# Order of loads, conversions and block requests in the first strip of a linear-attention and squared-ReLU MLP kernel

## The chip, the cores and the metric

The kernel runs on one core of a Trainium2 chip. The metric is the device time of one execution in microseconds. In the text PE is TensorE, DVE is VectorE, ACT is ScalarE, POOL is GpSimd and SP is SyncE, which here only issues DMAs.

## The reference

```python
kv = einsum('bhsd,bhse->bhde', k, v)        # q, k, v: (8, 8, 576, 64), float32
out = einsum('bhsd,bhde->bhse', q, kv)
rms = sqrt(mean(out * out, axis=-1, keepdims=True) + 1e-6)
x = (out / rms * g_norm)                    # heads joined: x is (4608, 512)
h = maximum(x @ w_in, 0.0)                  # w_in (512, 2048), float64
y = (h * h) @ w_out                         # w_out (2048, 512), float64
```

## The kernel before

**Tiling.** The 4608 tokens are cut into nine strips of 512 (`s` = 0 to 8). A strip has an up stage (x times `w_in`, squared ReLU into `gt`) and a down stage (times `w_out`, then a store). Strip 0 computes its up stage plainly (`up_first`, four matmuls of 512 columns for each of sixteen tiles) and its down stage with seven products in place of eight blocks (`down`, products 1 to 7, each in two halves; the order in strip 0 is 1, 2, 5, 6, 7, 3, 4). Strip 1 uses seven products in its up stage too, and from its down stage on each product is itself made of seven (`down_deep`, `up_slot`). These products need sums and differences of blocks of the weights and of x, which DVE and POOL make.

**Attention.** A batch has eight heads, taken as four pairs. For a pair, `transposed_query` (T) turns q on PE, `key_value` (K) multiplies k and v, and the query product follows. Its squares are summed (`mean_of`), ACT takes the root (`root_of`), DVE inverts it and takes a Newton step (`inverse_root`), and a multiply on DVE gives `x_n`, which PE transposes into `xT` (`features`).

**The opening.** The first 512 tokens, all of batch 0, go through steps of their own, listed by hand in `slices`: T, K, Q (`first_queries`: product, squares and mean), N (`first_normalized`: root, inverse and `x_n`), F (`first_features`), U (`first_up`: the first matmuls of the up stage), and for the weights `act` and `piece`. `w_in` and `w_out` come as float64 in pieces of 512 KB (`raw`). `convert_on_act` does two ACT operations on a piece, then `conversion` four DVE operations (L261, L263, L267, L270). `(piece, (i, n))` does the next n of these four for piece i. `keep_busy(ps, n)` makes n dummy matmuls (each two in the trace). Every engine runs its instructions in the order in which the program lists them.

**Loads.** Nearly all loads are issued by SP, in program order. `load(b, p, ...)` issues q, k and v of a pair, 256 KB each in batch 0; those of pairs 2 and 3 of batch 0 are put into a `gt` buffer (`first_qkv`). `load_piece` issues the next weight piece and `load_more` fills up to eight.

**Blocks of `w_out`.** The converted sums of `w_out` lie in DRAM. Products 1, 2 and 5 of strip 0 find their blocks in SBUF; for 6, 7, 3 and 4, in this order, `stream()` requests the next 1 MB block (`w_blk`, L824). It takes one of four buffers of `stream_pool`. `store_deep_sums(p, w)` makes four DVE sums of block p (`w_t`) for the deeper products of later strips and stores them (L857; those of product 6 use other buffers, L851). Its tiles come from the same four buffers. `deep_due` holds what is due, and the main loop empties it after each step except after one:

```python
while deep_due and i != n_up + 1:
    store_deep_sums(*deep_due.popleft())
```

In that loop `i - n_up` counts the halves of strip 0's down stage: 0 and 1 are product 1, 2 and 3 product 2, 4 and 5 product 5, 6 and 7 product 6, and so on. `attend` advances the `slices` of batch 1 between these steps; at `n_up + 5` it does the mean, root and norm of a pair of token tiles, whose `features` follow at `n_up + 7`.

Of the kernel before, what the change touches and what calls it, by code (L numbers as in the profile page):

```python
# [10 lines left out]
FP32 = mybir.dt.float32  # L11
# [9 lines left out]
def kernel(  # L21
# [34 lines left out]
    nc = tc.nc  # L56
    P = 128
# [4 lines left out]
    NP = H // 2  # L62
    FC = d_ff // P
    C = S // P
# [22 lines left out]
    g_pool = ctx.enter_context(tc.tile_pool(name="g", bufs=4))  # L87
# [10 lines left out]
    ctx.enter_context(tc.manual_schedule())  # L98


    main = {}

    def load(b, p, q_eng, names="kvq", parts=range(4)):
        hs = slice(2 * p, 2 * p + 2)
        inputs = (("q", q, q_eng), ("k", k, nc.sync), ("v", v, nc.sync))
        if b == 0 and p >= 2:

            h_place = g_pool.tile([P, 4, C * P], FP32, name="first_qkv", tag="gt")
        if b == 1 and p == 2:
            h_place = spare_pool.tile([P, 3, C * P], FP32, name="more_qkv")  # L110
        placed = (b, p) in ((0, 2), (0, 3), (1, 2))
        for i, (n, src, eng) in enumerate(inputs if b == 0 else inputs[1:] + inputs[:1]):
            if n not in names:
                continue
            whole = src[b, hs, 0 : C * P].rearrange("h (sp c) d -> sp h c d", c=C)
            if n == "q" and b >= Q_ON_PE:

                t = qkv_pool.tile([P, 4 * C, SQ], FP32, name=n, tag=n, bufs=3) if 0 in parts else main[n, b, p]
                for a in parts:
                    h, f = divmod(a * SQ, D)  # L120
                    eng.dma_start(
                        out=t[ts(a, SQ)],
                        in_=src[b, 2 * p + h, 0 : C * P, f : f + SQ].rearrange("(k i) f -> i k f", k=4 * C),
                    )
            elif n != "q":
                if placed:
                    t = h_place[:, i].rearrange("p (h c d) -> p h c d", h=2, c=C)
                else:
                    t = qkv_pool.tile([P, 2, C, D], FP32, name=n, tag=n)
                eng.dma_start(out=t, in_=whole)  # L130
            elif b == 0:

                if placed:
                    t = h_place[:, i].rearrange("p (h c d) -> p h c d", h=2, c=C)
                else:
                    t = qkv_pool.tile([P, 2, C, D], FP32, name=n, tag=n, bufs=3)
                eng.dma_start(out=t, in_=whole)
            else:

                if placed:  # L140
                    t = h_place[:, i].rearrange("p (c h d) -> p c h d", h=2, c=C)
                else:
                    t = qkv_pool.tile([P, C, 2, D], FP32, name=n, tag=n, bufs=3)
                for h in range(2):
                    eng.dma_start(out=t[:, :, h, :], in_=whole[:, h])
            main[n, b, p] = t
# [32 lines left out]
    to_load = iter(units)  # L179

    def load_next(q_eng=nc.sync, names="kvq"):
        u = next(to_load, None)
        if u is not None:
            load(*u, q_eng, names)
# [49 lines left out]
    def load_piece():  # L234
        if len(raw) < len(sources):
            t = raw_pool.tile([P, 2, WN // 2], I64, name="raw", tag="raw")
            nc.sync.dma_start(out=t, in_=sources[len(raw)])
            raw.append(t)
# [42 lines left out]
    def load_more(end):  # L281

        while len(raw) < min(end + 8, max(len(sources) - 4, end + 4), len(sources)):
            load_piece()
# [60 lines left out]

    load_next()
    load_rest(0, nc.sync)
    for p in range(1, NP):
        load_next()
        load_piece()  # L350
    load_more(0)
    g_col = const.tile([P, 1], FP32, name="g_col")
    g_src = g_norm.rearrange("(d u) -> d u", u=1)
# [13 lines left out]
    def keep_busy(ps, n):  # L367


        for _ in range(n):  # L370
            nc.tensor.matmul(ps, lhsT=ident, rhs=ident[:, : ps.shape[1]], start=True, stop=True)
# [38 lines left out]
    def key_value(b, *ps_of):  # L410
        while any(f == load and a[:2] == (b, p) or f == load_rest and a[0] == b for _, f, a in keys_due for p in ps_of):
            _, f, a = keys_due.popleft()
            f(*a)
        ps = apsum.tile([P, len(ps_of), D], FP32, name="kv_ps", tag="at")
        if (b, ps_of[0]) == (0, 0):
            keep_busy(ps[:, 0], 5)
            warm = apsum.tile([P, NT, P], FP32, name="x_ps", tag="first")[:, 0]
        half = slice(REST * (b % 2), REST * (b % 2 + 1))
        tiles = [[main.pop((n, b, p)) for n in "kv"] for p in ps_of]
        steps = [(i, c) for i in range(len(ps_of)) for c in range(C)] + [(i, C) for i in range(len(ps_of))]  # L420
        for i, c in steps:
            if (b, ps_of[i], c) == (0, 0, C):
                keep_busy(warm, 2)
            for h in range(2):
                at = (slice(None), h, c) if c < C else (half, 2 * ps_of[i] + h)
                a, w = (t[at] for t in (tiles[i] if c < C else (k_rest, v_rest)))
                nc.tensor.matmul(  # L427
                    ps[ts(h, D), i], lhsT=a, rhs=w, start=i == 0 and c == 0, stop=c == C, skip_group_check=True
                )
        at = (NP * b + ps_of[0]) % (2 * NP)  # L430
        d = kv_all[:, at : at + len(ps_of)]
        nc.scalar.copy(d[0:D, :, 0:D], ps[0:D])
        nc.scalar.copy(d[D:P, :, D:P], ps[D:P])
        for i, p in enumerate(ps_of):
            kvd[b, p] = d[:, i]
            if b < 2:
                if b == 1 and p == 0:
                    load_next()
            else:
                u = next(to_load, None)  # L440
                if u is not None:
                    keys_later(load, *u, nc.sync, "kv")
                if p == NP - 1 and b + 1 < B:
                    keys_later(load_rest, b + 1, nc.sync)
# [189 lines left out]
    slices, ready = [], {}  # L634
# [2 lines left out]
        convert_on_act, transposed_query, key_value, first_queries, first_normalized, first_features, first_piece  # L637
    )
    U = first_up
    slices += [(T, (0, 0)), (K, (0, 0)), (T, (0, 1)), (Q, (0,)), (K, (0, 1)), (N, (0,)), (act, (0,)), (piece, (0, 4))]  # L640
    slices += [(T, (0, 2)), (Q, (1,)), (F, (0,)), (K, (0, 2)), (N, (1,)), (act, (1,)), (U, (0, [0])), (piece, (1, 4))]
    slices += [(T, (0, 3)), (Q, (2,)), (F, (1,)), (U, (0, [1])), (K, (0, 3)), (N, (2,)), (act, (2,))]
    slices += [(Q, (3,)), (U, (0, [2])), (F, (2,)), (U, (1, [0])), (piece, (2, 1)), (N, (3,)), (act, (3,))]
    slices += [(piece, (2, 3)), (U, (1, [1, 2])), (F, (3,)), (piece, (3, 4))]
    slices += [(U, (2, [0, 1, 2])), (U, (3, [0, 1, 2]))]
    ready[0] = len(slices)
# [13 lines left out]
    T, K, last = transposed_query, key_value, query_pairs(1)[2]  # L660
# [198 lines left out]
    def down(s, p, i):  # L859
        if i == 0:  # L860
            open_bank(p)
        a = {1: 11, 2: 21, 6: 11, 7: 12, 3: 21, 4: 22}.get(p)
        w = w_blk[s, p]
        product(
            p, i,
            lambda fc: (gq[s, 1, fc // 2][:, fc % 2] if p == 5 else gq[s, a][:, fc])[:, ts(i, P)],
            lambda fc: w[:, :, fc], FQ,
        )

        if i == (p == 1) and s == DEEP - 1:  # L870
            deep_due.append((p, w))
        if i == 0:
            return
        del w_blk[s, p]

        if s == 0 and p in (2, 6, 3):
            reserve({2: 5, 6: 7, 3: 4}[p])
        if p not in (1, 7) and (s, p) not in ((0, 3), (0, 4)):
            stream()
        if p == (1 if s else 2):  # L880
            for g in range(NG):
                x = gq[s, 11][:, ts(g, 2)]
                minus(nc.vector, x, gq[s, 1, g], x)
        if p == (2 if s else 6):
            minus(nc.vector, gq[s, 21], gq[s, 21], gq[s, 11])

        def store(th, eh):
            def f(b, a=None):
                o = out_tile()
                if a is None:  # L890
                    nc.scalar.copy(o, b)
                else:
                    nc.vector.tensor_tensor(out=o, in0=b, in1=a, op=ALU.add)
                send(s, th, eh, o)
            return f

        combine(p, store(0, 0), store(0, 1), store(1, 0), store(1, 1))
# [284 lines left out]
    for s in range(N_STRIP):  # L1182
# [23 lines left out]
        for i, (w, fn, a) in enumerate(steps):  # L1206
# [53 lines left out]
                    stream()  # L1260
                continue
            if i == n_up:
                stream()
            if i == n_up + 3:
                store_first(2)
            if i in (n_up + 8, n_up + 11):
# [8 lines left out]
            n = i + 1 - (n_up - 6)  # L1275
            pairs, m = divmod(max(n - 2 * NP, 0), 3)
            attend(min(ready[0] + min(max(n, 0), 2 * NP) + (n >= 2 * NP) + 4 * pairs + (0, 2, 2)[m], goal))
            while deep_due and i != n_up + 1:
                store_deep_sums(*deep_due.popleft())
            if 11 <= i < n_up:  # L1280

# [31 lines left out]
```

## Time and profile before

| | us |
|---|---|
| median of 3 runs | 898.0 (897.18 to 898.66) |
| profiled execution, own time | 897.15 |
| its span | 895.1 |
| PE busy | 880.4 |
| DVE busy | 734.5 |
| ACT busy | 315.7 |
| POOL busy | 307.1 |
| DMA queue of SP, share of the 16 DMA engines' span | 81.2% |

The span runs from the first to the last instruction that the profiler saw; 2.05 us of the execution lie around it. Busy times are of one execution and overlap. All times named in the text as "at 118" are microseconds from the start of the span. The opening reaches to about 30 us, strip 0's up stage to 85, its down stage from 85 to 142, strip 1's up stage to 199.

### The profile page before, as it was taken

The numbers are of one execution on the slowest core, as the hardware profiler recorded it, in microseconds if no ns is written. First come the engines' busy times: TensorE is split into PE (matmuls) and PEld (weight loads), VectorE is DVE, ScalarE is ACT, GpSimd is POOL, SyncE is SP. The second block draws the span as 40 slices with busy tenths as digits, with TensorE's granted clock in tenths as the row PEclk, the third lists the DMA queues.
The fourth block names the chain that finished last, engine by engine and source line by source line (L and its number), as shares of the span: only waits on it lengthen the run. The fifth ranks groups of instructions, "written<-read, shape, count | busy, mean of one in ns | idle before, by whom it ended". The sixth has DMA issues, their size and how long they took to land.

```text
span 895.1 us, 20697 instructions
## 1 busy us (share of the span) xinstructions
PE 880.4 (98%) x8300; PEld 823.0 (92%) x8300; DVE 734.5 (82%) x1256; ACT 315.7 (35%) x622; POOL 307.1 (34%) x315
## 2 busy tenths in 40 slices
PE   8999999999999999999999999999999999999998
PEld 7445878889999999999999999999999999999998
DVE  3999999779779986898689966895899779875886
ACT  4798241320027302640255023801271027102710
POOL 0000005700558233632373035604460447044700
PEclk9999999999999999999999999999999999999999
DMA  9998998999988798969877989798748865884384
GB/s 303 307 316 250 310 330 267 289 314 323 313 197 279 266 326 238 277 249 317 250 232 238 323 239 248 237 297 292 218 143 297 304 203 164 301 299 154 128 316 180
DMA packets 169231, 235.71 MB, mean 263 GB/s; under 512 B 79408, under 2 KB 134192, under 8 KB 160688
## 3 DMA queue, kind: packets, MB, share of 16 engines
q1 hardware_dynamic: 168976, 234.40, 81.2%
q8 instruction: 65, 1.06, 0.5%
q14 instruction: 30, 0.25, 0.1%
q10 hardware_dynamic: 160, 0.00, 0.0%
HBM read 197.66 MB, written 36.70 MB: 262 GB/s over the span
## 4 chain that ended last, share of the span: by engine, by line
PE 74%; DVE 13%; DMA 6%; issue 2%; ACT 2%; SPq 2%; DVEq 0%; ACTq 0%
PE ps_B L944 22%; PE ps_A L944 17%; PE ps_A L1132 15%; PE ps_B L1132 8%; PE ps_A L729 4%; PE ps_C L1132 3%; PE ps_B L729 2%; PE kv_ps L427 1%; DVE w_c L267 1%; PE x_ps L463 1%; DVE gt L1144 1%; DMA w_blk<-w_in_deep 1%; DVE w_t L287 1%; DMA v_rest<-in_v_dram 1%; DMA x_d<-x_q 1%
## 5 line engine op out<-in xcount | busy, mean ns | idle before, releaser
L944 PE MATMUL ps_B<-w_blk,g_s 128*128 128x128 f32 x1024 | 126.2, 275 | 0.0
L944 PEld LDWEIGHTS ps_B<-w_blk,g_s 128*128 128x128 f32 x1024 | 120.0, 192 | 0.2
L1132 PE MATMUL ps_A<-x_l,w_in 128*128 128x128 f32 x784 | 104.1, 276 | 0.0
L287 POOL TENSOR_TENSOR x_l<-xT 128x256 f32<-128x256 f32 x21 | 16.2, 769 | 246.4 <-PE ps_A L944 246.4
L944 PE MATMUL ps_B<-w_blk,gt 128*128 128x128 f32 x768 | 97.4, 275 | 0.0
L1132 PEld LDWEIGHTS ps_A<-x_l,w_in 128*128 128x128 f32 x784 | 95.4, 192 | 0.5 <-DVE gt L1144 0.2
L944 PE MATMUL ps_A<-w_blk,g_s 128*128 128x128 f32 x768 | 93.6, 275 | 0.0
L944 PEld LDWEIGHTS ps_B<-w_blk,gt 128*128 128x128 f32 x768 | 91.5, 192 | 0.1
L944 PEld LDWEIGHTS ps_A<-w_blk,g_s 128*128 128x128 f32 x768 | 89.6, 192 | 0.0
L1144 POOL TENSOR_TENSOR snap<-snap,gt 128x512 f32<-128x512 f32 x35 | 46.6, 1332 | 118.9 <-ACT snap L1149 54.7
L1149 ACT COPY snap<-ps_A 128x512 f32<-128x512 f32 x63 | 36.7, 583 | 133.5 <-PE ps_A L1132 119.5
L1082 ACT ACTIVATE gt<-gt 128x512 f32<-128x512 f32 x112 | 69.6, 622 | 18.1 <-DVE gt L1144 18.0
L959 DVE TENSOR_TENSOR o_sb<-o_sb,ps_B 128x256 f32<-128x256 f32 (+1 forms) x128 | 49.5, 387 | 30.9 <-ACT o_sb L960 19.2
L944 PE MATMUL ps_A<-w_blk,gt 128*128 128x128 f32 x576 | 72.3, 275 | 0.0
L1083 ACT ACTIVATE gt<-gt 128x512 f32<-128x512 f32 x112 | 70.6, 631 | 3.6
L944 PEld LDWEIGHTS ps_A<-w_blk,gt 128*128 128x128 f32 x576 | 68.2, 192 | 0.4 <-DMA w_blk<-w_deep 0.2
L1144 POOL TENSOR_TENSOR gt<-gt,snap 128x512 f32<-128x512 f32 x42 | 52.6, 1278 | 23.8 <-DVE snap L1144 23.7
L287 DVE TENSOR_TENSOR gt<-gt 128x2048 f32<-128x2048 f32 (+1 forms) x29 | 59.7, 2063 | 0.0
L1042 POOL TENSOR_TENSOR w_i<-w_in 128x512 f32<-128x512 f32 x7 | 9.7, 1382 | 142.2 <-DVE w_in L287 141.5
L960 ACT COPY o_sb<-ps_A 128x128 f32<-128x128 f32 x24 | 6.4, 266 | 146.2 <-PE ps_A L944 146.2
L1132 PE MATMUL ps_A<-x_l,w_blk 128*128 128x128 f32 x392 | 52.2, 276 | 1.3 <-issue 1.2
L1132 PE MATMUL ps_B<-x_l,w_blk 128*128 128x128 f32 x392 | 52.0, 276 | 0.0
(180 smaller groups left out, 1811.7 us busy)
## 6 DMA issues: line engine op xcount, KB each, us to landing
w_blk<-w_deep SPq DMA_DIRECT2D x56, 1024.0 KB, 6.8
w_blk<-w_out SPq DMA_DIRECT2D x56, 768.0 KB, 6.0
w_blk<-w_in_deep SPq DMA_DIRECT2D x49, 768.0 KB, 4.8
raw<-in_moe_w_in_dram SPq DMA_DIRECT2D x16, 512.0 KB, 7.4
raw<-in_moe_w_out_dram SPq DMA_DIRECT2D x16, 512.0 KB, 6.2
k<-in_k_dram SPq DMA_DIRECT2D x29, 256.0 KB, 4.8
v<-in_v_dram SPq DMA_DIRECT2D x29, 256.0 KB, 5.0
x_d<-x_q SPq DMA_DIRECT2D x27, 256.0 KB, 5.3
```

The source lines that it names most:

```text
L267: yield nc.vector.scalar_tensor_tensor(out=ci, in0=high, scalar=-(2**30), in1=ci, op0=ALU.bitwise_and, op1=ALU.bitwise_or)
L287: eng.tensor_tensor(out=out, in0=a, in1=b, op=ALU.subtract)
L427: nc.tensor.matmul(ps[ts(h, D), i], lhsT=a, rhs=w, start=i == 0 and c == 0, stop=c == C, skip_group_check=True)
L729: nc.tensor.matmul(bank[BANK[p]][:, i, :], lhsT=lhsT(k), rhs=rhs(k), start=p in (1, 5, 2) and i == 0 and k == 0, stop=k == n - 1, skip_gro ...
L944: nc.tensor.matmul(chain[c][x][:, i, :], lhsT=a[:, f, :], rhs=w[:, f, :], start=x not in opened[c] and f == 0, stop=f == FQ // 2 - 1, skip ...
L959: add = lambda out, a, b: nc.vector.tensor_tensor(out=out, in0=a, in1=b, op=ALU.add)
L1042: nc.gpsimd.tensor_tensor(out=s1, in0=w_half(b, 0, 1), in1=w_half(b, 1, 1), op=ALU.add)
L1082: nc.scalar.activation(o, o, AF.Relu)
L1083: nc.scalar.activation(o, o, AF.Square)
L1132: nc.tensor.matmul(ps[:, i, :], lhsT=w, rhs=rhs, start=j in (1, 2, 5) and i == 0, stop=True, skip_group_check=True)
L1144: add = lambda eng, out, a, b: eng.tensor_tensor(out=out, in0=a, in1=b, op=ALU.add)
L1149: nc.scalar.copy(t, ps)
```

## The change

It has six parts. `load` remembers the `gt` buffer of a pair, so that q can be loaded apart from k and v. The first loads of pair 1 are no longer followed by a weight piece; for pairs 2 and 3 the order becomes q, piece, k and v in place of q, k, v, piece. The dummy matmuls before the first `key_value` go from five calls to three. In `slices`, the last DVE step of pieces 0 and 1 is put behind the mean of the next pair, and three of the `U` steps move. In strip 0's down stage two blocks are requested at `n_up` in place of one, one more at `n_up + 6`, and none any more in `down` of products 5 and 6. The loop no longer makes deep sums after step `n_up + 4`; they follow a step later, after that step's `attend`.

```diff
-    main = {}
+    main, first_places = {}, {}
...
         if b == 0 and p >= 2:
-            h_place = g_pool.tile([P, 4, C * P], FP32, name="first_qkv", tag="gt")
+            if p not in first_places:
+                first_places[p] = g_pool.tile([P, 4, C * P], FP32, name="first_qkv", tag="gt")
+            h_place = first_places[p]
...
     load_next()
     load_rest(0, nc.sync)
-    for p in range(1, NP):
-        load_next()
+    load_next()
+    for p in range(2, NP):
+        load(0, p, nc.sync, "q")
         load_piece()
+        load(0, p, nc.sync, "kv")
+        next(to_load)
     load_more(0)
...
-            keep_busy(ps[:, 0], 5)
+            keep_busy(ps[:, 0], 3)
...
-    slices += [(T, (0, 0)), (K, (0, 0)), (T, (0, 1)), (Q, (0,)), (K, (0, 1)), (N, (0,)), (act, (0,)), (piece, (0, 4))]
-    slices += [(T, (0, 2)), (Q, (1,)), (F, (0,)), (K, (0, 2)), (N, (1,)), (act, (1,)), (U, (0, [0])), (piece, (1, 4))]
-    slices += [(T, (0, 3)), (Q, (2,)), (F, (1,)), (U, (0, [1])), (K, (0, 3)), (N, (2,)), (act, (2,))]
-    slices += [(Q, (3,)), (U, (0, [2])), (F, (2,)), (U, (1, [0])), (piece, (2, 1)), (N, (3,)), (act, (3,))]
+    slices += [(T, (0, 0)), (K, (0, 0)), (T, (0, 1)), (Q, (0,)), (K, (0, 1)), (N, (0,)), (act, (0,)), (piece, (0, 3))]
+    slices += [(T, (0, 2)), (Q, (1,)), (F, (0,)), (K, (0, 2)), (piece, (0, 1)), (N, (1,)), (act, (1,)), (piece, (1, 3))]
+    slices += [(T, (0, 3)), (U, (0, [0])), (Q, (2,)), (F, (1,)), (U, (0, [1])), (K, (0, 3)), (piece, (1, 1)), (N, (2,))]
+    slices += [(act, (2,)), (U, (0, [2])), (Q, (3,)), (F, (2,)), (U, (1, [0])), (piece, (2, 1)), (N, (3,)), (act, (3,))]
...
-        if p not in (1, 7) and (s, p) not in ((0, 3), (0, 4)):
+        if p not in (1, 7) and (s, p) not in ((0, 5), (0, 6), (0, 3), (0, 4)):
             stream()
...
             if i == n_up:
-                stream()
+                stream(2)
...
-            while deep_due and i != n_up + 1:
+            if i == n_up + 6:
+                stream()
+            while deep_due and i not in (n_up + 1, n_up + 4):
                 store_deep_sums(*deep_due.popleft())
```

## The prediction

> **What bounds the kernel now.** I read the page's busy times first, then PE's waits, longest first (engine and what it writes, what it waited for; us in total, times, longest). PE is busy 98% of an 895.1 us span, so only its holes can give time:
>
> ```profile
> PE 880.4 (98%) x8300; PEld 823.0 (92%) x8300; DVE 734.5 (82%) x1256; ACT 315.7 (35%) x622; POOL 307.1 (34%) x315
> ```
>
> ```profile
> PE ps_A L576 <- DVE w_in L270: 1.8, 2, 1.1
> PE xt_ps L591 <- DVE x_n L531: 1.3, 2, 1.0
> PE ps_B L729 <- DVE w_in L287: 1.0, 1, 1.0
> PE t_ps L399 <- DMA first_qkv<-in_q_dram: 0.8, 1, 0.8
> PE x_ps L541 <- ACT kv_all L433: 0.5, 1, 0.5
> ```
>
> The reader sees that five waits of 5.4 us in all lie where the diff works: 1.8, 0.8 and 0.5 in the opening, 1.0 (of the 1.3) and 1.0 in the first strip's down stage. The third is misnamed: the block for product 3 is requested at 117.72 and takes 10.3 us, so it lands at 128.02, and PE starts at 128.16. It waits for that DMA. Next the windows, for what lies beside PE between the two places:
>
> ```profile
> 44.00:52.00 8.00, 8.00 (x20) 3.56 (x19) 8.00 (x18) 7.55 (x16) 0.00 (x0) 1.00 1.11 314
> 52.00:60.00 8.00, 8.00 (x20) 3.59 (x19) 8.00 (x19) 7.67 (x17) 0.00 (x0) 1.00 0.98 365
> 112.00:120.00 8.00, 7.04 (x36) 5.81 (x36) 7.44 (x16) 2.29 (x4) 0.00 (x0) 1.00 1.05 352
> ```
>
> After the stretch and its length come PE, PE's loads, DVE, ACT, POOL, clock, DMA share and GB/s. From 44 to 60 us four resources are full at once (PE 8.00 of 8, DVE 8.00, ACT 7.6, DMA about 1): time won earlier must get past each of them. From 112 to 120 PE loses 0.96 while DVE is at 7.44 of 8. The timeline shows how tight that is:
>
> ```profile
> 53.61 0.68 ACT L249 ACTIVATE w_c<-raw 128x512 f32<-128x512 f32 x1
> 55.40 0.66 ACT L777 ACTIVATE gt<-ps_B 128x256 f32<-128x256 f32 x2
> 56.39 3.60 PE L770 MATMUL ps_B<-xT,w_in 128*128 128x512 f32 x8
> ...
> 153.44 0.69 DVE L792 TENSOR_TENSOR gt<-ps_A,snap 128x512 f32<-128x512 f32 x1 [0.48 <-PE ps_A L729]
> ...
> 158.85 0.63 PE L591 MATMUL xt_ps<-ident,x_n 128*128 128x128 f32 x4 [0.34 <-DVE x_n L531]
> ```
>
> A PE tile of the first strip can start only when ACT has emptied the bank used four tiles before: ACT ends at 55.40 + 0.66 = 56.06, PE starts at 56.39, slack 0.33. And DVE, full from 26 us, first waits for PE at 153.44; at 158.85 PE waits for DVE.
>
> **What the skill says.** "TensorE: Matmul & The Clock Gate", What's actually happening: PE starts at half clock and is released after some 3.4 us of activity, in free-running windows. The trace agrees: the dummy matmuls start 0.21 us apart until 7.23 us, then 0.11. "DMA: Bandwidth & Descriptors", Anatomy of one DMA: about 2.0 us fixed plus bytes over 436 GB/s, for 1 MB an estimate of 4.4 us (stated for another issuing path). Block 6, which lands alone, took 4.8; I use 4.8. "SBUF — State Buffer", SBUF: two separate sides: DVE with two SBUF inputs and POOL lock each other out. Agrees: 128x512 sums on DVE take 0.68 us, but 1.64 to 1.76 once POOL starts at 143.75.
>
> **The opening, by step.** (a) Two keep_busy calls fewer are four dummy matmuls, the last of ten, already at full clock: 4 x 0.11 = 0.44 us. Their successors have their data (v of pair 0 by 1.74 + 4.4 = 6.1). So key_value(0,0), and behind it everything to the mean of pair 0, comes 0.44 sooner. (b) q of pair 2 landed at 6.76 + 6.6 = 13.36 behind a 512 KB piece. Ahead of it, it lands between 10.7 (256 KB took 0.7 just before) and 11.9, and PE can take its transpose at 12.25: the 0.79 hole goes. The piece takes the old place of q, about 13.35. ACT began its two operations on that piece at 13.52 anyway, and stands there in order. I take no cost; to bound it, 1 us later would hold up ACT, not DVE, which is still busy with the first norm. Count and bytes of the DMAs stay. (c) Splitting the pieces moves the last conversion step (L270, 0.6 net) of pieces 0 and 1 behind the next mean. By the rows of the timeline (mean 0.69 + 0.17, root 0.21, four Newton steps 0.9, product 0.69, each piece step 0.43 to 0.69, FIFO per engine) DVE's normalizing products (L548) start at 14.11, 18.6, 23.75 and 26.85 instead of 14.55, 19.59, 24.78 and 28.01: 0.44, 0.99, 1.03 and 1.16 sooner. U(0,[0]) behind the transpose of pair 3 costs PE nothing: it waits for L270 at 17.75 as before, but with that transpose done. The hole at 23.13 is filled by U(0,[2]). **DVE leaves the opening 1.15 us sooner** (0.8 to 1.5), PE too, since it waits for DVE's last pieces.
>
> **The middle.** ACT does not keep the 1.15: pieces 16 and 17 land at 45.05 + 7.2 = 52.25 and 45.70 + 7.8 = 53.5, ACT takes them at 52.36 and 53.61, and DMA has no gap before. So PE keeps 0.33 (bounds 0.3 and 1.15, if landings move too). DVE keeps all: act of piece 17 ends its first operation at 54.29 and DVE wants it at 56.03, 1.7 us of slack.
>
> **The first strip's down stage.** (d) The four sums for product 5 (112.89 to 115.42, 2.53 us) go behind the norm. x_n, ready at 119.46, is ready at about 116.9 - 1.15 = 115.8; PE comes at 118.04 - 0.33. The 0.97 hole goes. DVE's total is the same. Queued behind the moved sums are those of product 6, which keep their place, and the store of 5's sums, 2.8 us later (118.3 for 115.53). (e) Blocks 6 and 7 are requested together at 102.4, block 3 in place of 7, block 4 one step after the norm. Four buffers exist, and sums for 1 and 2 fill the other two: block 3 must wait for the store of the second sums (landed at 108.79 + 4.8 = 113.6), so it lands at about 113.6 + 4.8 = 118.4 to 120, needed at 126. The 1.02 hole goes. Block 4 waits at the head of SP's queue for that store, which lands at 124 to 126 behind 2.25 MB; block 4 then lands at about 130, needed at 132.8. Behind it on SP stand four stores of 6's sums and the loads of k, v and q for pair (2,0), which landed by 136.8 and are first used at 148.15. Moved SP issues cost 0.3 to 1.2 us each, hidden by PE's 7 us per product. PE is then 0.33 + 0.97 + 1.02 = 2.3 us ahead.
>
> **What is late next.** DVE is only 1.15 ahead when strip 1 begins. Its wait of 0.48 at 153.44 shrinks to nothing and gives 0.44 more; so x_n for 158.85 comes 1.15 + 0.44 = 1.6 sooner and PE, 2.3 ahead, waits. Beyond it PE has 3.6 us of holes to the end (the same list of waits from 160 us on), none owed to the edits. v of the fourth pair of batch 2 lands at 157.17 + 5.0 = 162.2, used at 162.87; the second block of strip 1's deep stage lands at 193.55 + 7.9 = 201.45, used at 202.07. Both have 0.6 us of slack and SP, held by DVE's sums at 137.85, moves with DVE: 0.6 + 1.15 > 1.6.
>
> **Sum.** The profiled execution took 897.15 (2.05 around the span) and would take 895.55. It lies 0.85 under the median of 898.0, so I say 898.0 - 1.6 = **896.4**. A measurement can tell about 0.2%, 1.8 us, from no change.
>
> **Rivals.** *Forecast, 0.45:* DVE's gain decides; 1.6, own range 0.7 to 2.5, 895.5 to 897.3. *All of PE's gain, 0.22:* a different buffer for POOL's first sum lets DVE finish the sums for block 4 before the lock-out (up to 3 us of it), or pieces land sooner; then 2.3 to 3.1, about 895.3. For it: DVE's lateness at 153 is three sums at 1.7 instead of 0.68. Against: POOL's start follows DVE's. *The gain stops at a DMA, 0.18:* the loads of 162 and 201 don't move and leave 0.6, about 897.4; DMA share near 1 from 150 speaks for it. That the change does not ask sooner belongs here: held by buffers, block 3 gains only 4 us of request. *Slower, 0.15:* block 4's wait for the store of 5's sums blocks SP. It decides from the point where that store lands after 128.0 (132.8 - 4.8); a store has taken 8.3 us in this place. At 131 the block lands at 136 to 139.7, PE waits 3 to 7 us, and 2.3 of gain leave 1 to 4.5 of loss: about 900. Against: 7's load, 1 MB, is out of the way.
>
> **Chances.** Faster by over 0.2% (below 896.2) is rival two and nearly half of the forecast, 0.22 + 0.22 = 0.44; within it 0.23 + 0.18 = 0.41; slower 0.15. The range 894.8 to 899.4 leaves out under a tenth at the bottom and about a tenth of slow cases.
>
> **What would show it.** Right: no wait of t_ps L399 for q; x_n L548 at 14.1 and 26.9; no holes before xt_ps near 117.7 and ps_B near 126; PE's tile at 56.39 only 0.3 sooner; a hole of about 1 us before xt_ps near 157.3. Wrong: dummy matmuls cut while the clock is still low; ACT's tile at 56 a full us sooner; a PE wait for w_blk near 133; SP idle over 8 us before block 4.

## Result and profile after

The changed kernel took **901.61 us** (median of 20 runs, 898.16 to 903.75), the kernel before 898.98 (20 runs beside them, 897.18 to 901.41). The ratio is 1.0025, 95% interval 1.0014 to 1.0035: about 2.2 us slower (the medians differ by 2.6), where 1.6 faster was forecast. The profiled execution took 899.97 with a span of 897.9, which is 2.8 longer than before.

The page's busy times and PE's waits (longest first: us in total, times, longest):

```profile
PE 880.6 (98%) x8296; PEld 822.8 (92%) x8296; DVE 734.4 (82%) x1256; ACT 315.6 (35%) x622; POOL 306.5 (34%) x315
```

```profile
PE kv_ps L431 <- DMA v_rest<-in_v_dram: 3.3, 2, 3.0
...
PE ps_A L580 <- DVE w_in L271: 1.1, 1, 1.1
PE xt_ps L569 <- DVE x_n L552: 1.0, 2, 0.5
PE xt_ps L595 <- DVE x_n L535: 0.5, 1, 0.5
PE ps_A L774 <- ACT gt L781: 0.5, 1, 0.5
PE ps_A L580 <- DVE rms L495: 0.5, 1, 0.5
PE ps_A L733 <- DVE o_sb L897: 0.3, 1, 0.3
```

Work is the same but for four dummy matmuls; only holes moved. The waits that the change was to remove have gone: the two of 1.0 in the down stage, q of pair 2, the one for ACT (`kv_all`), and one of the two on w_in. The opening has three new ones of about 0.5 each (for x_n and rms). The large new one, 3.05 us, is for v_rest of batch 2 (the values of the last 64 of its 576 tokens). The timelines of PE and DVE show where it comes from (start, us, line, operation, in brackets the idle time before it and what ended it). PE in the changed kernel, then in the kernel before:

```profile
145.98 1.15 PE L431 MATMUL kv_ps<-v,k 128*64 128x64 f32 x32
150.18 0.45 PE L431 MATMUL kv_ps<-v_rest,k_rest 64*64 64x64 f32 x8 [3.05 <-DMA v_rest<-in_v_dram]
150.56 3.12 PE L733 MATMUL ps_B<-x_t,w_in 128*128 128x256 f32 x8
153.47 2.49 PE L733 MATMUL ps_A<-x_t,w_in 128*128 128x256 f32 x8
155.80 1.89 PE L733 MATMUL ps_B<-xT,w_in 128*128 128x256 f32 x8
...
161.69 0.63 PE L595 MATMUL xt_ps<-ident,x_n 128*128 128x128 f32 x4 [0.55 <-DVE x_n L535]
```

```profile
148.15 1.15 PE L427 MATMUL kv_ps<-v,k 128*64 128x64 f32 x32
149.23 0.45 PE L427 MATMUL kv_ps<-v_rest,k_rest 64*64 64x64 f32 x8
149.61 1.99 PE L729 MATMUL ps_B<-x_t,w_in 128*128 128x256 f32 x8
151.44 1.89 PE L729 MATMUL ps_A<-x_t,w_in 128*128 128x256 f32 x8
153.17 1.89 PE L729 MATMUL ps_B<-xT,w_in 128*128 128x256 f32 x8
```

DVE in the changed kernel, and its last line here in the kernel before:

```profile
114.25 1.29 DVE L535 TENSOR_TENSOR x_n<-x_ps,newton 128x512 f32<-128x512 f32 x2
116.64 0.69 DVE L288 TENSOR_TENSOR w_t<-w_in 128x512 f32<-128x512 f32 x1 [1.10 <-DMA w_deep<-w_t]
...
125.73 1.29 DVE L288 TENSOR_TENSOR w_in<-w_in 128x512 f32<-128x512 f32 x2 [0.41 <-DMA w_out<-w_in]
...
138.52 0.68 DVE L288 TENSOR_TENSOR x_t<-xT 128x512 f32<-128x512 f32 x1
```

```profile
138.34 0.68 DVE L287 TENSOR_TENSOR x_t<-xT 128x512 f32<-128x512 f32 x1
```

PE reaches the K step of batch 2 at 145.98 (148.15 before), 2.17 sooner. There it stands still for 3.05, and the two groups behind the hole run below full clock: 5.24 us from 150.56 to 155.80, where before they took 3.56 (149.61 to 153.17), so 1.68 is lost. With 0.07 in the K step and 0.21 more of waiting for x_n (0.55 for 0.34), -2.17 + 3.05 + 1.68 + 0.07 + 0.21 = 2.84 = 161.69 - 158.85. Behind that PE's waits are those of before, and the 2.8 stay to the end. The clock is seen in the windows (stretch, length, PE, loads, DVE, ACT, POOL, clock, DMA share, GB/s):

```profile
148.00:152.00 4.00, 1.82 (x13) 1.59 (x14) 3.93 (x5) 0.52 (x2) 3.24 (x3) 0.91 0.39 72
152.00:156.00 4.00, 4.00 (x13) 3.27 (x13) 1.13 (x2) 0.69 (x2) 3.84 (x4) 0.66 0.98 346
```

DVE's story is as short. It is 1.38 ahead at the norm of 101.03 (102.41 before) and 1.39 ahead at 110.90 (o_sb, the output that DVE makes from PE's banks; 112.29 before). Then it waits 1.10 for the store of product 2's sums, whose tile the sums of product 5 are to take, and 0.41 for a store of a part of `w_in` (`store_first(2)`, L329) that it is to overwrite. At 138.52 it is 0.18 behind (138.34 before).

SP, which issues nearly every transfer in program order, stands between the two. It never has more than eight of its transfers under way in these traces. First the changed kernel, then two lines of the kernel before:

```profile
114.24 0.32 SPq L828 DMA_DIRECT2D w_blk<-w_out  x1
...
122.46 0.37 SPq L828 DMA_DIRECT2D w_blk<-w_out  x1
...
135.09 0.91 SPq L861 DMA_DIRECT2D w_deep<-w_t  x1
...
138.03 0.33 SPq L861 DMA_DIRECT2D w_deep<-w_t  x1
...
140.41 1.31 SPq L131 DMA_DIRECT2D v<-in_v_dram  x1
...
144.82 1.79 SPq L161 DMA_DIRECT2D k_rest<-in_k_dram  x1
146.66 0.63 SPq L161 DMA_DIRECT2D v_rest<-in_v_dram  x1
```

```profile
134.39 0.88 SPq L857 DMA_DIRECT2D w_deep<-w_t  x1
...
144.50 0.63 SPq L160 DMA_DIRECT2D v_rest<-in_v_dram  x1
```

k and v of pair (2,1) and the rest keys and values of batch 2 (`load_rest(2)`) stand behind the stores of the sums of products 7 and 3. v_rest, issued at 146.66 (144.50 before), takes 3.4 and lands at 150.0. Before it landed at 148.3 and was used at 149.23: 0.9 of slack, for a PE that was to come 2 us sooner. So the hole has two parts: 1.3 us of it would be there if v_rest landed when it did before, and 1.7 come from its landing 1.7 later. DVE's lateness is the smaller part of those 1.7: the store of 138.03 goes out as soon as DVE has made the sums, 0.18 later than before. The store ahead of it goes out 0.70 later (135.09 for 134.39) although DVE had its sums ready at 132.2; SP stood there behind the loads of q, the second of which (131.94) went out only as block 4 landed (131.9). The rest is added while the transfers stand behind each other.

### The profile page after: what moved, and what is told of

It reads as the page before. It is cut to its first block, busy times and chain, and to the rows that moved or that the text cites. A ratio compares the mean times of both kernels' runs of the same rounds, so it can differ in the third digit from the quotient of the medians.

```text
span 897.9 us, 20684 instructions
## 1 busy us (share of the span) xinstructions
PE 880.6 (98%) x8296; PEld 822.8 (92%) x8296; DVE 734.4 (82%) x1256; ACT 315.6 (35%) x622; POOL 306.5 (34%) x315
## 4 chain that ended last, share of the span: by engine, by line
PE 78%; DVE 13%; DMA 3%; issue 2%; SPq 1%; ACT 1%; DVEq 0%; ACTq 0%
PE ps_B L948 22%; PE ps_A L1136 17%; PE ps_A L948 17%; PE ps_B L1136 9%; PE ps_C L1136 4%; PE ps_A L733 2%; PE kv_ps L431 2%; DVE w_c L268 2%; PE x_ps L467 2%; PE ps_B L733 2%; DMA w_out<-w_in 1%; DVE w_t L288 1%; DVE wt L288 1%; DVE w_in L288 1%; DVE w_in L271 1%
```

## The experiments

**Theory 1:** from 104 to 150 us stores and loads stand one behind the other in SP's queue and on the DMA engines; PE, sooner by 2 us, meets the loads at their end, and the half clock adds to it. **Rival A:** the opening's edits cost. **Rival B:** DVE's two waits for stores are the root. Ratios to the kernel before (12 to 22 runs of each kernel, 5 of a4 and 6 of b1):

| kernel | ratio | 95% interval |
|---|---|---|
| the change | 1.0025 | 1.0014 to 1.0035 |
| a1 rest loads sooner by four steps | 1.0025 | 1.0016 to 1.0033 |
| a2 PE kept busy in the hole | 1.0032 | 1.0021 to 1.0043 |
| a3 opening alone | 0.9997 | 0.9986 to 1.0007 |
| a4 down stage alone | 1.0048 | 1.0036 to 1.0060 |
| c1 rest loads at 98 us | 1.0007 | 0.9994 to 1.0020 |
| c2 and pair (2,0) at 98 us | 1.0025 | 1.0014 to 1.0037 |
| d1 c2 and 5's sums elsewhere | 1.0018 | 1.0007 to 1.0029 |
| c3 before, with c2's loads | 1.0002 | 0.9991 to 1.0014 |
| g1 change less output stores | 0.9983 | 0.9973 to 0.9993 |
| g2 before less output stores | 0.9995 | 0.9983 to 1.0007 |
| e1 c1, 5's sums elsewhere, one store sooner | 0.9979 | 0.9968 to 0.9990 |
| b1 requests alone | 1.0041 | 1.0027 to 1.0055 |
| h1 e1 without moved rest loads | 0.9987 | 0.9979 to 0.9995 |
| h2 e1 without the opening | 0.9992 | 0.9979 to 1.0006 |
| h3 change, 5's sums elsewhere | 1.0023 | 1.0014 to 1.0032 |

### Which half of the change loses (a3, a4)

a3 has the opening's edits (loads, dummies, `slices`) on the kernel before; a4 the other hunks, `stream` and `deep_due`.

> The kernel before with only the edits of the opening (order of q loads and pieces, three dummy calls in place of five, the order of the slices). Theory 1: DVE leaves the opening 1.4 us sooner and PE 0.3 (ACT's bank at 56 us), the wait for x_n at 118 shrinks by about 1 us, but PE then waits longer for block 3 near 127, which DMA lands at 127 to 128 as before. In all 0 to 0.5 us faster than before. Rival A (the opening costs the time): 2 us slower than before. Rival C (DVE's whole 1.4 us reaches the end): 1.4 us faster.

> The kernel before with only the edits of strip 0's down stage (blocks asked for sooner, sums for product 5 behind the norm). Theory 1: both waits of PE at 118 and 127 go, DVE waits for the stores and is then about 1 us later than before, v_rest of batch 2 lands about 2 us later than before, PE waits for it 3 us or a little more, and its clock falls: 2.5 to 3.5 us slower than before, as slow as the changed kernel. Rival A (the opening costs the time): 1 to 2 us faster than before.

a3 is no slower than before and a4 is 0.48% slower, more than the 2.5 to 3.5 us expected. The loss is in the down stage; rival A falls: with the opening's edits the loss is smaller (1.0025), not larger. a4's profile has three holes where the changed kernel has the one of 3.05: 1.8 for o_sb at 134, 1.5 for v and 1.7 for v_rest at 150 and 152.

### The late load by itself (a1, a2)

a1:

```diff
+            if i == n_up + 8:
+                load_rest(2, nc.sync)
             if i in (n_up + 8, n_up + 11):
                 load_next()
             if i == n_up + 12:
-                load_rest(2, nc.sync)
                 load_q_rest(2, nc.sync)
```

> The changed kernel with one edit: the loads of k_rest and v_rest of batch 2 are issued four steps sooner, ahead of k, v and q of pair (2,0). Theory 1 (the loss is PE's 3.05 us wait for v_rest at 147, and the half-clock matmuls behind it): the hole goes, PE reaches 158 us about 2 us ahead, and then stands until DVE's x_n. DVE lost its lead at 116.6 and 125.7, so x_n comes only 0.3 us sooner than in the kernel before: about 0.3 us faster than before, nearly 3 us faster than the changed kernel. Rival A (the new opening costs the time): still 2 us or more slower than before. Rival B (DVE's waits for stores, 1.1 and 0.4 us, are the loss): the hole goes, but a wait for x_n of over 2.5 us takes its place and the time stays about 2 us above before.

No time came back; theory 1's expectation missed, and so did rival B's (a wait for x_n). In its profile PE waits at the same K step, for v of the pair in place of v_rest:

```profile
PE kv_ps L431 <- DMA v<-in_v_dram: 3.2, 2, 2.6
```

The load that was put ahead lands in time, and the one that it was put ahead of is late: the queue is full there. In this execution, the fastest of a1's 18 (898.84, median 900.96), DVE waits 0.1 for the first store, not for the second, and makes at 137.52 the `x_t` of 138.34. v is late all the same, so late loads need no late DVE. a2 leaves the order and fills the hole with 24 dummy matmuls:

```diff
+        if (b, ps_of[0]) == (2, 0):
+            warm = fpsum.tile([P, P], FP32, name="warm_ps", tag="f")
...
+            if (b, ps_of[i], c) == (2, 0, C):
+                keep_busy(warm, 12)
```

> The changed kernel with twelve dummy matmul calls (24 matmuls of 128 columns, about 2.6 us at full clock) on PE where it waits for v_rest of batch 2, into a PSUM bank that nothing reads. Theory 1 with a clock part (PE's idle 3 us lets its clock fall to half, and the matmuls after the hole lose 1.7 us): the wait for v_rest stays where it was in time, the products behind it take 1.99 and 1.89 us instead of 3.12 and 2.49, and the time is 1.5 to 2 us below the changed kernel, still about 1 us above before. Rival (the slow products behind the hole have another cause, DVE or PSUM): they stay slow and the time stays that of the changed kernel.

```profile
148.32 0.69 PE L435 MATMUL kv_ps<-v,k 128*64 128x64 f32 x16 [1.15 <-DMA v<-in_v_dram]
148.93 2.94 PE L375 MATMUL warm_ps<-ident 128*128 128x128 f32 x24
151.81 0.45 PE L435 MATMUL kv_ps<-v_rest,k_rest 64*64 64x64 f32 x8
152.18 1.99 PE L737 MATMUL ps_B<-x_t,w_in 128*128 128x256 f32 x8
154.01 1.89 PE L737 MATMUL ps_A<-x_t,w_in 128*128 128x256 f32 x8
```

The groups behind the dummies run at full clock, 1.99 and 1.89 where they took 3.12 and 2.49. Yet the time does not fall, against the 1.5 to 2 us expected: v was late as well in this execution and the dummies ran some 0.9 us past v_rest. The half clock is real, but what it costs the whole kernel this run does not show: filling the hole brought nothing back.

### Loads into an idle stretch (c1, c2, c3, d1)

SP stands from 98.1 to 101.9. The request for block 6 waits there for the last of the stores to `w_out`, which lands at 101.8, and in the changed kernel the DMA share falls to 0.24:

```profile
100.00:104.00 4.00, 4.00 (x20) 3.51 (x19) 3.76 (x10) 0.00 (x0) 0.00 (x0) 1.00 0.24 77
```

c1 puts the rest loads there:

```diff
             if i == n_up:
+                load_rest(2, nc.sync)
                 stream(2)
...
             if i == n_up + 12:
-                load_rest(2, nc.sync)
```

> The changed kernel with the loads of the rest keys and values of batch 2 (two DMAs, 128 KB each) moved ahead of block 6's request, into a stretch in which SP stands from 98.1 to 101.9 us and the DMA share falls to 0.24. Theory 1 (from 104 to 150 us the loads and stores stand one behind the other in SP's queue of eight and on the DMA engines, PE's lead meets their end): the hole of 3.05 us at 150.18 goes; what is left is v of pair (2,1), which landed at 146.24 there, 0 to 1.2 us late. 0 to 1 us slower than before, 1.5 to 2.5 faster than the changed kernel. Rival B (DVE's two waits for stores, 1.5 us, decide): as slow as the changed kernel, +2 to +3 against before.

1.0007: within the range of theory 1, outside rival B's 2 to 3 us slower. The intervals of c1 and of the change overlap, though. No wait for v_rest is left in its profile (897.62, next to the fastest of 14), 0.7 for v and 1.0 for o_sb are. c2 puts pair (2,0) there too and (2,1) into its old place; c3 does the same to the kernel before; d1 adds to c2 the sums of product 5 in the pool of sums:

```diff
-        if p == 6:
+        if p in (5, 6):
             parts = [sum_pool.tile([P, FQ // 2, P], FP32, name=f"w_t{i}", tag="sum") for i in range(4)]
...
-        if s == 0 and p in (2, 6, 3):
-            reserve({2: 5, 6: 7, 3: 4}[p])
+        if s == 0 and p in (6, 3):
+            reserve({6: 7, 3: 4}[p])
```

> As the run before, and k, v and q of pair (2,0) too go into that stretch (six DMAs, 768 KB), and those of pair (2,1) take the place of (2,0). Theory 1: no PE hole between 132 and 158 beyond 0.4 us, no half clock; PE then waits for x_n near 158 as before the change, because DVE has spent its lead on waits for stores (which grow: blocks 6 and 7 and the stores behind them land up to 2.3 us later). 0.5 faster to 1 us slower than before. Rival B: DVE's waits alone make it +2 to +3, as the changed kernel.

> The kernel before with the same moved loads (rest keys and values and pair (2,0) ahead of block 6's request). Control: PE waited for no such load there, so both theories say within 0.7 us of before; if blocks land later for it, the hole at 128.16 grows by up to 1 us.

> As the run before, and the sums of product 5 are made in the pool of sums, as those of product 6 are, so that DVE needn't wait for the store of product 2's sums. Theory 1: DVE keeps its 1.4 us, PE its 2 us as far as x_n near 158; 1 to 2 us faster than before. Rival B gives the same here. If it is no faster than before, a limit that neither theory names stands behind 150 us.

c3 is as expected, although DVE waits 1.9 for a store in it: such a wait alone doesn't make the kernel before slower. c2 and d1 are not as expected, and DVE's waits say why; c2 first, then d1:

```profile
DVE w_t L288 <- DMA w_deep<-w_t: 4.8, 1, 4.8
DVE w_in L288 <- DMA w_out<-w_in: 2.0, 1, 2.0
```

```profile
DVE w_in L288 <- DMA w_out<-w_in: 4.9, 1, 4.9
```

With the megabyte ahead of blocks 6 and 7 (768 KB and the rest) the stores behind them land later (that of product 2's sums at 120.7 in c2, for 116.6), DVE's two waits grow from 1.5 to 6.8 us, and PE waits for DVE's o_sb: 2.8 in c2, 4.0 in d1; in c2 it also waits 2.0 for a block. (c2's profiled execution, 903.04, is 2.35 above its median.) That is rival B's mechanism: late stores hold DVE, and DVE holds SP and PE. With the first wait gone (d1), 4.9 of the 6.8 turn up at the second.

### Less traffic in the stage (g1, g2)

> The changed kernel without the stores of the first strip's outputs (256 KB each; three of them lie ahead of the loads of pair (2,1) and of the rest, 0.7 to 1.5 us of the DMA each). Its output lacks that strip. Theory 1 (the stage from 104 to 150 us is full of transfers and the change moves PE ahead of them): v of pair (2,1) and v_rest land about 2 to 2.5 us sooner, the hole of 3.05 shrinks to under 1; 1.5 to 2.5 us faster than the changed kernel, and within 0.7 of the kernel before with the same stores left out. Rival B (DVE's wait of 1.1 for product 2's sums decides): that store lies ahead of the first output store, the wait stays, still 2 us slower than the kernel before with the stores left out.

> The kernel before without the stores of the first strip's outputs; its output lacks that strip. Control for the run before. PE waited there for one block alone (1.02 us), which would land 0.7 sooner: 0.3 to 1 us faster than before by both theories.

With the edit `if s == 0: return` in `send`, the change is no longer the slower of the two: 0.9983 over 0.9995 is 0.9988, 1.1 us, with intervals that overlap. The hole for v_rest is 1.5 in place of 3.05 (theory 1 said under 1). But DVE's waits have gone too, which rival B did not expect; the profiled execution is the fastest of 21. So this pair shows that with less traffic the loss goes, and does not tell theory 1 from rival B.

### The requests alone (b1)

> The kernel before with the sooner requests for blocks alone (sums of product 5 stay ahead of the norm, opening unchanged). The hole of 1.02 at 128 goes, that of 0.97 at 119 stays. Theory 1: PE is 1 us ahead at 147 and the loads are 0.5 to 1.5 later, so a hole of 0.5 to 1.5 there: 0 to 1.5 slower than before. Rival B: the sums of product 5, asked for sooner than in the changed kernel, wait longer for the store of product 2's sums (landed at 116.6, wanted at 113), 3 us or more, and behind them x_n: 2 to 4 slower.

```profile
DVE w_t L287 <- DMA w_deep<-w_t: 3.6, 1, 3.6
...
PE xt_ps L591 <- DVE x_n L531: 4.7, 1, 4.7
```

Rival B's numbers: DVE waits 3.6 for the store of product 2's sums, and the norm stands behind it. By the buffers' addresses the sums of product 5 take product 1's tile in the kernel before and product 2's with the new requests, since one more block holds a buffer. The traces agree: these sums start at 112.89 before, when the store of product 2's sums has not landed (113.6), and in b1 at 116.41, when it just has (116.4). Putting the sums behind the norm leaves 1.1 of these 3.6. It does not remove the wait.

### Both causes met (e1), and one at a time (h1, h2, h3)

e1 is c1 with d1's edit, and the store of `w_in` a step sooner. That puts it ahead of block 3's request and also of the stores of the sums of products 1 and 2: SP issues it at 102.75, for 115.08 in the changed kernel:

```diff
-            if i == n_up + 3:
+            if i == n_up + 2:
                 store_first(2)
```

> The changed kernel with both theories' costs met: rest keys and values of batch 2 loaded in the stretch from 98 to 102 us, the sums of product 5 in the pool of sums, and the store of W_in's first half that DVE waited 0.41 us for issued a step sooner, ahead of block 3. If late loads (theory 1) and DVE's waits (rival B) are all, 0.5 to 1.5 us faster than before. If the stage is full whatever the order, what is moved ahead makes something else late: 0 to 1.5 slower, with a PE wait for o_sb or for v near 132 to 147.

> The changed kernel with the sums of product 5 in the pool of sums and nothing else. DVE's wait of 1.1 us at 116.6 goes; it then comes to W_in's sums at about 124.2, whose old contents are stored by a DMA that landed at 125.6, and waits 1.4 there in place of 0.4. Nothing of DVE's time comes back: as slow as the changed kernel, 1.5 to 3 slower than before. If it comes back all the same, within 0.7 of before.

> The changed kernel with the sums of product 5 in the pool of sums and the store of W_in's first half a step sooner; the rest keys and values of batch 2 stay where they were, behind pair (2,1). If DVE's two waits (1.5 us) are the root of the late loads (the stores of sums and the loads stand behind DVE's results in SP's queue): hole at K(2,0,1) under 0.7 us, 1 to 1.8 faster than before. If the rest loads are late by themselves: they land at about 148.5 to 149.5, wanted at 147.2, hole of 1.3 to 2.3: within 0.7 of before.

> The fastest version so far without the opening's edits. By the prediction's step the opening leaves PE 0.33 us ahead and DVE 1.15; PE holes at 118 and 128 gone: 2.0 less 0.3 to 0.4. If DVE's lead from the opening counts (x_n at 157 is late by DVE), only 0.5 to 1 faster than before; if PE's alone counts, 1.3 to 1.7 faster.

**e1 beats both kernels:** 0.9979, 1.9 us under the kernel before (medians 896.95 and 898.70), a little more than expected. From 100 to 165 us PE waits once in its profile:

```profile
PE xt_ps L595 <- DVE x_n L535: 0.3, 1, 0.3
```

PE takes x_n at 156.92 (158.85 before), 1.9 sooner at the place where the prediction wanted 1.6. That this equals the 1.9 of the medians is chance. In this execution the lead is lost again by 202, most of it in a wait of 0.45 for DVE's qT at 165.7 and at the block of 202. e1 first, then before:

```profile
202.02 1.16 PE L948 MATMUL ps_B<-w_blk,gt 128*128 128x128 f32 x8 [0.56 <-DMA w_blk<-w_deep]
```

```profile
202.07 1.06 PE L944 MATMUL ps_B<-w_blk,gt 128*128 128x128 f32 x8
```

The execution ends 0.7 sooner than the profiled one of before (spans 894.4 and 895.1). h1's profile loses its lead of 1.8 in the same way, at 167. How the medians keep what the profiles lose there is not shown.

h3 takes away DVE's first wait alone and changes nothing, since the second grows in its place, and PE waits in the steps where it waits in the change, and for v too:

```profile
DVE w_in L288 <- DMA w_out<-w_in: 1.7, 1, 1.7
...
PE kv_ps L431 <- DMA v<-in_v_dram: 1.9, 1, 1.9
PE kv_ps L431 <- DMA v_rest<-in_v_dram: 1.8, 1, 1.8
PE ps_A L733 <- DVE o_sb L897: 1.3, 1, 1.3
```

h1 differs from h3 by the one moved store. DVE then waits for no store, the store of product 3's sums, which SP issues as DVE ends them, goes out at 136.29 for 138.55, v_rest lands at 147.7 for 151.5, and the ratio falls from 1.0023 to 0.9987, some 3.2 us. Holes of 1.8 for v_rest and 0.5 for v are left, as the second of its expectations says, but the time is within that of the first. The four kernels side by side:

| | rest loads in place | rest loads at 98 us |
|---|---|---|
| DVE's waits left | 1.0025 (the change) | 1.0007 (c1) |
| DVE's waits removed | 0.9987 (h1) | 0.9979 (e1) |

So **DVE's two waits carry most of the loss**: without them the kernel is faster in both columns, by 0.38 and 0.28%, and the intervals do not overlap. Moving the rest loads is worth 0.08 to 0.18%, which the intervals do not separate from nothing. Theory 1 is not refuted by this: loads remain late in h1 and a1 without DVE's waits. The edits that remove the waits also change the order of the stores, and what that alone is worth was not tried. Of the opening, too, the intervals do not decide: 0.9992 without it (h2), 0.9979 with it.

## Why the prediction was wrong

**The opening held.** The starts of x_n (L548, now L552) were forecast to within 0.4: the timeline has 13.81, 18.24, 23.37 and 26.60. PE's tile of 56.39 starts at 56.04, 0.35 sooner where 0.33 was forecast, and ACT takes the weight piece of 53.61 at 53.55: pinned by its DMA, as said. That the size fits is in part luck: with the same opening this tile starts at 56.79 in e1's profile and at 54.84 in h1's. Four dummies fewer brought the first K step to 6.76 from 8.11, more than the 0.44 counted, and it then waited 0.25 for v. PE ran at full clock from 4.60 in this execution (the transposes there took 1.09 for 1.98) and from 7.23 before.

**The down stage's first half held.** The holes at 118 and 128 are gone, PE is 2.17 ahead against 2.3. Block 4, the rival *slower*, did not do it: it was requested at 122.46, as soon as SP had issued the store ahead of it, took block 6's buffer and landed at 131.9 for 132.8. That rival's figure of about 900 came near to the time by luck, since its wait never arose.

**The step that failed first is (d):** "DVE's total is the same." The working counted DVE's operations and put its waits at nothing. It gave the tile of the moved sums no thought, although (e) had counted the four buffers and used the store of "the second sums" to price block 3. In the changed kernel block 3 takes the tile of product 1's sums (that store lands at 114.2, the request goes out at 114.24), and product 5's sums take the one of the second. Its store was forecast to land at 113.6 and landed at 116.6 (9.2 us from its issue, for 4.8 before); block 7's megabyte, which was requested behind it, now goes ahead of it. DVE came for the tile at 115.5 and waited 1.10. The store of `w_in`, which now has block 3's megabyte ahead of it as well, brought the second wait, 0.41. "DVE is only 1.15 ahead when strip 1 begins" was mis-sized by these waits: 1.39 less 1.51, so 0.1 to 0.2 behind.

**The second is in "What is late next".** Two loads are named there, of 162 and 201, with 0.6 us of slack each. The load with 0.9 of slack at 149.23 lay nearer, in the way of a PE 2.2 ahead, and was left out: step (e) ends its list of what is behind SP at pair (2,0) and does not reach (2,1) and the rest. That alone is worth the 1.3 us of hole above. "SP, held by DVE's sums at 137.85, moves with DVE" held for that one store, but the loads behind it did not gain the 1.15 that was booked; v came 1.5 and v_rest 1.7 later. The rival *the gain stops at a DMA* had the right kind of cause, for the change at the wrong place, and no price for PE's standing still: 3.05 of hole cost 1.68 more in clock. In e1, where the other losses are away, the block that it named stops the lead at 202.

A slip in the working bears on nothing: the five waits named at its start make 5.1 us, not 5.4.

## What to carry to other kernels

When a request is moved ahead in a full queue, list what it is put in front of, and ask of each store there which engine waits to overwrite its source. Here the store behind a block asked for 7 us sooner landed 3 us later, and DVE waited for it with all that it had yet to do. Before a gain of x us is booked, list every load used in the next stage with its slack: all with less than x are the next bound. And a wait taken away can turn up at the next store: removing DVE's first wait by itself was worth nothing (h3), and one more store moved by one step of the loop was then worth 3 us (h1).

## What was not expected of the hardware

"TensorE: Matmul & The Clock Gate" of the Trainium skill, HAM oscillation, wants no idle gaps of PE over about 3.4 us, lest its clock fall. Here shorter ones did it: 3.05 us in the changed kernel (clock 0.91 and 0.66 in the next stretches of 4 us), and 2.76 in c2:

```profile
136.00:140.00 4.00, 1.40 (x6) 1.21 (x7) 3.90 (x8) 0.00 (x0) 0.00 (x0) 0.95 1.05 348
140.00:144.00 4.00, 4.00 (x13) 3.27 (x12) 3.97 (x7) 0.00 (x0) 0.00 (x0) 0.62 0.86 282
```

In a4 two holes of 1.5 and 1.7 with 0.7 of work between them were enough (0.73 and 0.50), while a1's 2.59 left the clock at 1.00. The measurement decides: here a hole of 2.8 or 3.05 us cost its length and 1.7 us more (in c2 the product behind it took 8.86 for 7.17).

"DMA: Bandwidth & Descriptors", Queues, rings and completion order, says that an engine's descriptors are consumed in ring order, and warns that completion need not follow the order of issue. In this trace it did: in the changed kernel all of SP's transfers from block 6's request at 101.9 on landed in the order of their issue. So v_rest, 128 KB, landed behind the 64 KB loads of q and the 1 MB stores that it was put behind.
